# Attention with a gated convolution: the first query chunk of the first batch shares its weights with the last two chunks; tile 24 of v and small loads of v are fetched in another way

## The chip, the cores and the metric

The kernel runs on one core of one Trainium2 chip. The metric is the device time of one execution in microseconds (us), the median of several runs; lower is better. The engines are named as the profile names them: PE is TensorE with PEld for its weight loads, DVE is VectorE, ACT is ScalarE, POOL is GpSimd, and SP is SyncE, which here only issues DMA transfers (rows "SPq"). Every engine works through its own instructions strictly in order.

## The reference

Eight batches of 3200 rows. Per batch the scores of z with itself are scaled, cut off at zero and squared; this symmetric 3200 x 3200 matrix multiplies v, the result is multiplied by u, and the product x passes through a gate (a causal convolution of five taps and a sigmoid) and two 256 x 256 matrices:

```
scores = (1 / S) * z @ z.T            # z: 8 x 3200 x 64
attn   = maximum(scores, 0) ** 2      # symmetric
x      = u * (attn @ v)               # u, v: 8 x 3200 x 256
gate   = sigmoid(causal_conv5(x, conv_w))
out    = (gate * (x @ w_val)) @ w_out
```

## The kernel before

**Precision.** Every factor of a product is split into a high part, rounded to the format that PE takes, and a low part, the difference. A product is three matmuls (low x high, high x low, high x high). The names ending in `h`/`l` or `hi`/`lo`, and `v_hl` and `zhl`, which hold both, are these parts.

**Tiling.** The 3200 rows are 25 tiles of 128. Queries are handled in six chunks of four tiles (512 queries, `c` = 0 to 5), and the 25th tile (`ONE`) runs beside chunk 5. Keys are taken in pairs of tiles, `i` = 0 to 12; pair 12 is the single tile 24. Pairs 2c and 2c+1 lie in chunk c. One **step** is one (batch, chunk, pair).

**A step.** PE makes the scores of a step three steps ahead (`scores`, six matmuls into a bank `s`). `weights_of` turns them into weights: ACT cuts off and scales (L640, out of `s` into a buffer `a`, of which there are two), squares (L641) and rounds to `ah` (L643); DVE subtracts to get `al` (L649). Three steps later PE multiplies `ah` and `al` with v into the two banks `acc` (`attend`, 24 matmuls). All PE matmuls of a step have line L428 or L733, the helpers.

**Turned blocks.** Because the matrix is symmetric, the block (keys of chunk g, queries of chunk c) is the transpose of a block needed later, when chunk g is the query chunk. Where `keeps(b, c, g)` says so, `turn` has DVE transpose `a` into a tile `turned` (L520; two buffers) behind `al`, `keep` writes it to DRAM as `mir` (L542, four DMAs of SP), and in chunk g `m_fetch` reads it back into a tile `m` (L551, L555; four buffers). Such a **fetched** step has no scores, no L640 and no L641; ACT casts `ah` straight from `m`. Fetches are issued six or seven steps ahead. In batches 1 to 7 every chunk keeps blocks for all later ones. In batch 0 chunk 0 keeps only the block for `ONE`, and chunk 1 those for chunks 2 and later.

**Order of the steps.** `MIRRORED_AT` and the mixes place fetched steps between computed ones. In batch 0 chunk 4 computes pairs 0, 1, 8, 10, 11, 12 and half of 9 and fetches 2 to 7; chunk 5 computes 12, 0, 10, 1 and half of 11 and fetches 2 to 9 and the three groups of `ONE` (`FIRST_MIX`; K is the single pair, O the own pairs, F fetched, C other computed, S a group of `ONE`). In batches 1 to 6 chunk 4 fetches 0 to 7 in one run of six and two more, and chunk 5 fetches 0 to 9 (`LAST_MIX`).

**Order of the rest.** Everything else is put at steps by hand: `at_step(s, fn, ...)`. For v: `v_load` reads it from DRAM (L356, four DMAs of 32 partitions each), `v_high` rounds it (L410, on DVE in batch 0 but for pair 1, on ACT later), `v_low` subtracts (L415, DVE). `V_LOAD` and `V_HIGH` hold the steps for batches 1 and up, counted from the start of chunk 5 of the batch before; tile 24 is read three steps in and rounded six steps in. In batch 0 `v_load_chunk` reads v of chunks 2 to 5 into the two `turned` buffers. z of the next batch is loaded by `Z_FROM`, counted from the start of that batch. `convert` and `convert_conv` turn the weights, given as 64-bit numbers, into 32-bit ones on DVE, in pieces spread over the first 25 steps, with temporaries in the `m` buffers.

**Between chunks.** When a chunk's last step is done, DVE multiplies both banks with u (`gated`, L763); the next chunk's matmuls into `acc` wait for that.

**The end.** The last chunk of the last batch is cut into a left and a right half of 256 columns, each for two halves h of the channels, behind `if s == END`; the code there is written out in the order in which each engine runs it.

Of the kernel before, what the change touches and what calls it, by code (L numbers as in the profile page):

```python
# [12 lines left out]
P = 128  # L13
# [4 lines left out]
def attn_glu_kernel(  # L18
# [260 lines left out]
    def keeps(b, c, g):  # L279

        return c < g and (b > 0 or c > 1 or (c == 1 and g >= 2) or g == ONE)
# [10 lines left out]
    FIRST_MIX = "KCOFFSCFFSFOSFFF"  # L292
# [3 lines left out]
    for b in range(B):  # L296
        for c in range(n_chunks):
# [5 lines left out]
            if c == n_chunks - 1:  # L303
                mix = FIRST_MIX if b == 0 else LAST_MIX[b == B - 1]
# [4 lines left out]
                    "C": [i for i in computed if i < own(c, 0)],  # L309
# [42 lines left out]
    def v_rows(dst, b, g, t, m):  # L352

        for a in range(P // BLK):
# [31 lines left out]
    def v_load_chunk(b, g):  # L386
        if g % 2 == 0:
            two[0] = sb.tile([P, 2, CW // P, D], F32, name="v_raws", tag="turned", bufs=2)
        v_load(b, range(firsts[g], firsts[g] + sizes[g]), two[0][:, g % 2])
# [22 lines left out]
    def v_low(b, i):  # L412
        for j, m, raw in v_parts(b, i):
            high, low = (vt[b, i][:, x, j : j + m] for x in range(2))
            nc.vector.tensor_tensor(low, raw, f32(high), op=ALU.subtract)  # L415
# [462 lines left out]
    def gate_part_low(b, c, e, cols, gv):  # L878
        gvh, gvl = (x[:, e, cols] for x in gvs[b, c])
        nc.vector.tensor_tensor(gvl, gv, f32(gvh), op=ALU.subtract)  # L880
# [427 lines left out]
    def fill_at(s, fn, *args):  # L1308
# [26 lines left out]
    Z_FROM = {b: (-53, -48, -41, -33, -22, -10, -15) if b > 1 else (-17, -40, -35, -31, -24, -9, -5) for b in range(1, B)}  # L1335
# [8 lines left out]
        (3, (24,), (1, 6)),  # L1344
# [3 lines left out]
        (16, (18, 19), None),  # L1348
    )
    V_HIGH = (7, 8, 9, 10, 11, 12, 13, 16, 17, 18, 14, 15, 6)  # L1350
# [120 lines left out]
    with tc.manual_schedule():  # L1471
# [13 lines left out]
        for s in range(min(todo), END + 1):  # L1485
# [86 lines left out]
            if s == END:  # L1572
# [7 lines left out]
                for cols in (left_, right):  # L1580
                    for h in range(DH):
# [6 lines left out]
                        else:  # L1588
                            nc.vector.tensor_tensor(sums[h], apart[h][:, : CW // 2], sums[h], op=ALU.add)
                            gated(b, c, h, cols, sums[h])  # L1590
                        x_high(b, c, one[h], cols)
# [7 lines left out]
                        conv(b, c, h, 0, nc.scalar.mul if (cols is left_) == (h == 1) else nc.vector.tensor_scalar_mul, cols)  # L1599
# [10 lines left out]
                for h in range(DH):  # L1610
                    value_part(b, c, h, left_, value_l)
                value_part(b, c, 0, right, value_r)
# [3 lines left out]
                project_whole(b, c - 1, two_banks(False))  # L1616
# [6 lines left out]
                for e in range(DH):  # L1623
                    gate_part_low(b, c, e, left_, lefts[e])
# [13 lines left out]
                project_tiles(b, c, (2, 3), rights)  # L1638
                one_project_whole(g, s_bank_pair(1 - next_s[0]))
                tiles_out(b, c, (2, 3), rights, ("ut", "turned"), (nc.vector.tensor_copy, nc.scalar.copy), (nc.scalar, nc.scalar))  # L1640
                one_out(g)

# [32 lines left out]
```

## Time and profile before

| | us |
|---|---|
| median of three runs | 2258.09 |
| the three runs | 2257.62, 2263.52, 2258.09 |
| the profiled execution, its own time | 2262.12 |
| its span in the profile | 2260.3 |
| busy: DVE | 1852.5 |
| busy: ACT | 1707.4 |
| busy: POOL | 76.6 |

The granted clock of PE is 1.00 in all but the last stretch of the trace. A row of the timeline gives the start, the duration, the engine, the line in the kernel, the operation with its tiles, and in brackets how long the engine stood idle before it and what ended that. Durations of neighbouring rows of one engine overlap a little, so distances from start to start say what an instruction costs its engine.

### The profile page before, as it was taken

The page shows a single profiled execution, that of the slowest core. Times are in us where ns is not written, and L with a number is a line of the kernel's source. Part 1 is how long each engine was busy: PE and PEld are TensorE (multiplying, and loading weights), DVE is VectorE, ACT ScalarE, POOL GpSimd, SP SyncE. Part 2 cuts the span into 40 slices and gives each one's busy share as a digit, 9 for nine tenths or more (in the row PEclk, how much of TensorE's full clock was granted, in tenths as well). Part 3 has the DMA queues.
Part 4 walks back from the last instruction along what each step waited for, and adds up shares of the span by engine and source line. Part 5 has one row for each costly group of instructions (what it writes and reads, how often), then busy time and mean ns, then how long its engine had stood idle before and what let it go on. Part 6 is the DMA issues. An engine that isn't in the chain of part 4 may idle for free.

```text
span 2260.3 us, 50037 instructions
## 1 busy us (share of the span) xinstructions
PE 2247.4 (99%) x20311; PEld 1911.3 (85%) x20311; DVE 1852.5 (82%) x2296; ACT 1707.4 (76%) x2145; POOL 76.6 (3%) x119
## 2 busy tenths in 40 slices
PE   9999999999999999999999999999999999999998
PEld 7888888889888988888988888888898888888888
DVE  8877788887889778887888968888788887888776
ACT  8987688766887668876688766987669776697764
POOL 0000000000000000000000000000000000000000
PEclk9999999999999999999999999999999999999999
DMA  5557857887677876788667776777858778677663
GB/s 123 117 135 159 205 136 164 184 197 205 150 163 181 189 200 150 169 185 193 182 164 168 189 185 177 166 177 183 206 144 184 173 181 206 148 184 172 170 179 98
DMA packets 700600, 386.61 MB, mean 171 GB/s; under 512 B 411856, under 2 KB 635088, under 8 KB 700368
## 3 DMA queue, kind: packets, MB, share of 16 engines
q1 hardware_dynamic: 699024, 383.01, 71.4%
q8 instruction: 159, 2.61, 0.5%
q14 instruction: 73, 0.60, 0.1%
q10 hardware_dynamic: 1344, 0.39, 0.1%
HBM read 211.82 MB, written 171.44 MB: 170 GB/s over the span
## 4 chain that ended last, share of the span: by engine, by line
PE 92%; SPq 2%; DVE 2%; DMA 2%; ACT 1%; issue 1%; ACTq 0%; DVEq 0%
PE acc L428 67%; PE s L428 12%; PE misc L428 11%; DMA m<-mir 1%; SPq L356 1%; DVE al L649 1%; PE acc L733 1%; SPq L161 1%; SPq L1044 0%; DVE gate L811 0%; DMA z_raw<-in_z_dram 0%; DMA v_raws<-in_v_dram 0%; ACT ah L643 0%; SPq L555 0%; DVE x L763 0%
## 5 line engine op out<-in xcount | busy, mean ns | idle before, releaser
L428 PE MATMUL acc<-ah,v_hl 64*128 64x512 f32 x9472 | 1606.9, 388 | 1.2 <-DVE x L763 0.6
L428 PEld LDWEIGHTS acc<-ah,v_hl 64*128 64x128 f32 x9472 | 942.9, 184 | 165.0 <-issue 1.5
L428 PE MATMUL acc<-al,v_hl 64*128 64x512 f32 x4736 | 965.0, 387 | 2.1 <-DVE al L649 2.0
L428 PEld LDWEIGHTS acc<-al,v_hl 64*128 64x128 f32 x4736 | 480.9, 184 | 83.6 <-DVE al L649 4.8
L649 DVE TENSOR_TENSOR al<-a,ah 128x1024 fp32r<-128x1024 f32 (+1 forms) x346 | 398.3, 1151 | 184.5 <-ACT ah L643 182.7
L640 ACT ACTIVATE a<-s 128x1024 f32<-128x1024 f32 (+1 forms) x346 | 333.0, 963 | 137.5 <-PE s L428 122.8
L643 ACT CAST ah<-m 128x1024 fp32r<-128x1024 f32 x254 | 264.9, 1047 | 154.4 <-PE acc L428 83.0
L641 ACT ACTIVATE a<-a 128x1024 f32<-128x1024 f32 (+1 forms) x346 | 347.7, 1005 | 11.0
L649 DVE TENSOR_TENSOR al<-m,ah 128x1024 fp32r<-128x1024 f32 x254 | 307.8, 1212 | 53.7 <-ACT ah L643 53.6
L643 ACT CAST ah<-a 128x1024 fp32r<-128x1024 f32 (+1 forms) x323 | 319.9, 990 | 10.2
L520 DVE STREAM_TRANSPOSE turned<-a 128x1024 f32<-128x1024 f32 (+1 forms) x278 | 318.5, 1146 | 0.1
L811 DVE SCALAR_TENSOR_TENSOR gate<-x,cw,gate 128x512 f32<-128x512 f32 (+1 forms) x392 | 284.7, 726 | 4.9 <-ACT gate L809 1.1
L428 PE MATMUL s<-zq,zhl 64*128 64x512 f32 (+1 forms) x1596 | 222.5, 378 | 1.6 <-DVE gv L1065 1.6
L428 PEld LDWEIGHTS s<-zq,zhl 64*128 64x128 f32 x1596 | 153.0, 184 | 30.0 <-DVE gv L1065 2.0
L763 DVE TENSOR_TENSOR x<-acc,ut 128x512 f32<-128x512 f32 (+1 forms) x96 | 61.4, 681 | 83.4 <-PE acc L428 70.5
L815 ACT ACTIVATE gate<-gate 128x512 f32<-128x512 f32 (+1 forms) x98 | 60.9, 622 | 71.1 <-DVE gate L811 70.8
L913 ACT CAST gvh<-gv 128x512 fp32r<-128x512 f32 x94 | 58.2, 620 | 38.0 <-DVE gv L909 37.9
L428 PE MATMUL misc<-xh,w_val_hi 64*128 64x512 f32 x376 | 77.2, 386 | 0.0
L428 PE MATMUL misc<-xh,w_val_lo 64*128 64x512 f32 x376 | 77.2, 386 | 0.0
L428 PE MATMUL misc<-xl,w_val_hi 64*128 64x512 f32 x376 | 77.2, 386 | 0.0
L428 PE MATMUL s<-v_hl,ah 64*128 64x512 f32 x400 | 76.3, 394 | 0.0
L909 DVE TENSOR_TENSOR gv<-misc,gate 128x512 f32<-128x512 f32 x94 | 64.5, 686 | 12.7 <-PE misc L428 8.3
(197 smaller groups left out, 2021.7 us busy)
## 6 DMA issues: line engine op xcount, KB each, us to landing
mir<-turned SPq DMA_DIRECT2D x460, 256.0 KB, 4.1
m<-mir SPq DMA_DIRECT2D x230, 512.0 KB, 4.9
u_raw<-in_u_dram SPq DMA_DIRECT2D x384, 64.0 KB, 3.5
mir<-turned SPq DMA_DIRECT2D x376, 64.0 KB, 2.5
m<-mir SPq DMA_DIRECT2D x94, 256.0 KB, 4.6
out_dram<-ob SPq DMA_DIRECT2D x152, 128.0 KB, 3.6
v_raws<-in_v_dram SPq DMA_DIRECT2D x100, 128.0 KB, 3.7
z_raw<-in_z_dram SPq DMA_DIRECT2D x182, 64.0 KB, 3.2
```

Of the source, the lines that this page charges most:

```text
L161: queues[i % len(queues)].dma_start(dst[i * BLK : (i + 1) * BLK], src[:, d0 : d0 + BLK].rearrange("(j c) r -> c j r", c=BLK),)
L428: ins = nc.tensor.matmul(out_, st[r], mv[r], start=first, stop=last)
L520: nc.vector.transpose(into[:, t : t + m], a[:, j * w : (j + m) * w].rearrange("p (t m x) -> p t m x", t=m, x=BLK))
L640: nc.scalar.activation(a[:, : n * w].rearrange("p (j x) -> p j x", j=2), s[:, :, :each], AF.Relu, scale=scale)
L641: nc.scalar.activation(a, a, AF.Square)
L643: nc.scalar.copy(hi, a)
L649: nc.vector.tensor_tensor(lo, a, f32(hi), op=ALU.subtract)
L763: nc.vector.tensor_tensor(x[:, h, HALO + cols.start : HALO + cols.stop], accs[b, c][h][:, cols] if with_ is None else with_, ut[b, c][:, h ...
L811: nc.vector.scalar_tensor_tensor(g, tap, cw[:, h, k : k + 1], g, op0=ALU.mult, op1=ALU.add)
L815: nc.scalar.activation(g, g, AF.Sigmoid)
L909: nc.vector.tensor_tensor(gv[:, :w], pvs[b, c][e][:, :w], gates[b, c][:, e, :w], op=ALU.mult)
L913: nc.scalar.copy(gvs[b, c][0][:, e, :w], gv_[b, c, e][:, :w])
```

## The change

- `keeps`: in batch 0 chunk 0 now also keeps its blocks for chunks 4 and 5. In chunk 0 pairs 8 to 11 are transposed (four more L520) and two blocks are written; chunks 4 and 5 fetch pairs 0 and 1. Both chunks then have the order of steps of batches 1 to 6, and `FIRST_MIX` goes.
- `v_load_chunk`: v of chunks 2 to 5 of batch 0 goes into `m` buffers, one per chunk.
- `v_rows`: a load of fewer than four tiles is one DMA per tile over 128 partitions, no longer four of 32 partitions.
- `v_low`: pairs 9 to 12 of batch 0 on POOL.
- Tile 24 of v in batches 1 to 7: read together with tiles 18 and 19 (step 16), rounded at step 19.
- `Z_FROM` of batch 1: z of chunk 0 two steps later, z of tile 24 fifteen steps earlier.
- The end: in two of the four parts the first tap runs on ACT ahead of the cast of x; `project_whole` moves ahead of the right half's value matmuls; two subtractions go to POOL; tile 2 and tile 3 are projected and stored apart, and tile 3 is copied by DVE.

```diff
-        return c < g and (b > 0 or c > 1 or (c == 1 and g >= 2) or g == ONE)
+        return c < g and (b > 0 or c > 1 or (c == 1 and g >= 2) or g >= 4)
...
-    FIRST_MIX = "KCOFFSCFFSFOSFFF"
...
-                mix = FIRST_MIX if b == 0 else LAST_MIX[b == B - 1]
+                mix = LAST_MIX[b == B - 1]
...
     def v_rows(dst, b, g, t, m):
 
+        if m < P // BLK:
+            for x in range(m):
+                k = firsts[g] * P
+                rows_ = v[b, k : k + sizes[g] * P, :].rearrange("(a t r) d -> t a r d", t=sizes[g], r=BLK)[t + x]
+                nc.sync.dma_start(dst[:, x], rows_)
+            return
...
     def v_load_chunk(b, g):
-        if g % 2 == 0:
-            two[0] = sb.tile([P, 2, CW // P, D], F32, name="v_raws", tag="turned", bufs=2)
-        v_load(b, range(firsts[g], firsts[g] + sizes[g]), two[0][:, g % 2])
+        v_load(b, range(firsts[g], firsts[g] + sizes[g]), sb.tile([P, CW // P, D], F32, name="v_raws", tag="m", bufs=4))
...
-            nc.vector.tensor_tensor(low, raw, f32(high), op=ALU.subtract)
+            (nc.gpsimd if b == 0 and i > 8 else nc.vector).tensor_tensor(low, raw, f32(high), op=ALU.subtract)
...
-    def gate_part_low(b, c, e, cols, gv):
+    def gate_part_low(b, c, e, cols, gv, engine=nc.vector):
         gvh, gvl = (x[:, e, cols] for x in gvs[b, c])
-        nc.vector.tensor_tensor(gvl, gv, f32(gvh), op=ALU.subtract)
+        engine.tensor_tensor(gvl, gv, f32(gvh), op=ALU.subtract)
...
-    Z_FROM = {b: (-53, -48, -41, -33, -22, -10, -15) if b > 1 else (-17, -40, -35, -31, -24, -9, -5) for b in range(1, B)}
+    Z_FROM = {b: (-53, -48, -41, -33, -22, -10, -15) if b > 1 else (-15, -40, -35, -31, -24, -9, -20) for b in range(1, B)}
...
-        (3, (24,), (1, 6)),
...
-        (16, (18, 19), None),
+        (16, (18, 19, 24), None),
     )
-    V_HIGH = (7, 8, 9, 10, 11, 12, 13, 16, 17, 18, 14, 15, 6)
+    V_HIGH = (7, 8, 9, 10, 11, 12, 13, 16, 17, 18, 14, 15, 19)
...
+                        on_scalar = (cols is left_) == (h == 1)
+                        if on_scalar:
+                            conv(b, c, h, 0, nc.scalar.mul, cols)
                         x_high(b, c, one[h], cols)
...
-                        conv(b, c, h, 0, nc.scalar.mul if (cols is left_) == (h == 1) else nc.vector.tensor_scalar_mul, cols)
+                        if not on_scalar:
+                            conv(b, c, h, 0, nc.vector.tensor_scalar_mul, cols)
...
+                project_whole(b, c - 1, two_banks(False))
                 value_part(b, c, 0, right, value_r)
...
-                project_whole(b, c - 1, two_banks(False))
                 lefts = [gate_part(b, c, e, left_, value_l, "a") for e in range(DH)]
...
-                    gate_part_low(b, c, e, left_, lefts[e])
+                    gate_part_low(b, c, e, left_, lefts[e], nc.gpsimd)
...
-                project_tiles(b, c, (2, 3), rights)
+                project_tiles(b, c, (2,), rights[:1])
+                tiles_out(b, c, (2,), rights[:1], ("ut",), (nc.vector.tensor_copy,), (nc.sync,))
                 one_project_whole(g, s_bank_pair(1 - next_s[0]))
-                tiles_out(b, c, (2, 3), rights, ("ut", "turned"), (nc.vector.tensor_copy, nc.scalar.copy), (nc.scalar, nc.scalar))
+                project_tiles(b, c, (3,), rights[1:])
                 one_out(g)
+                tiles_out(b, c, (3,), rights[1:], ("turned",), (nc.vector.tensor_copy,), (nc.scalar,))
```

The change adds seven lines above most of these places, so line numbers of the changed kernel are two higher in the middle of the program and more near its end.

Three places in the engines' orders follow. The first is DVE in batch 0, chunk 0, from the subtraction of pair 8 (`al`) on; `v_hl_513` and `v_hl_506` are v of pair 8, `v_hl_566` and `v_hl_562` that of pair 9, `cv_` names are those of the conversion. Before:

```order
L649 TENSOR_TENSOR al<-a,ah 128x1024
L215 STREAM_TRANSPOSE zz<-z_raw 128x128
L415 TENSOR_TENSOR v_hl_513<-v_raws,v_hl_513 128x512
L410 CAST v_hl_566<-v_raws 128x512
L106 TENSOR_SCALAR cv_rest<-cv_words_363 128x10
L108 SCALAR_TENSOR_TENSOR cv_rest<-cv_words_363,cv_rest 128x10
L649 TENSOR_TENSOR al<-a,ah 128x1024
L231 TENSOR_TENSOR zhl_611<-zz,zhl_611 128x128
L415 TENSOR_TENSOR v_hl_566<-v_raws,v_hl_566 128x512
L410 CAST v_hl_615<-v_raws 128x512
```

The same stretch of DVE now:

```order
L651 TENSOR_TENSOR al<-a,ah 128x1024
L522 STREAM_TRANSPOSE turned<-a 128x2x16x32
L215 STREAM_TRANSPOSE zz<-z_raw 128x128
L417 TENSOR_TENSOR v_hl_506<-v_raws,v_hl_506 128x512
L412 CAST v_hl_562<-v_raws 128x512
L106 TENSOR_SCALAR cv_rest<-cv_words_356 128x10
L108 SCALAR_TENSOR_TENSOR cv_rest<-cv_words_356,cv_rest 128x10
L651 TENSOR_TENSOR al<-a,ah 128x1024
L522 STREAM_TRANSPOSE turned<-a 128x2x16x32
L231 TENSOR_TENSOR zhl_608<-zz,zhl_608 128x128
L412 CAST v_hl_612<-v_raws 128x512
```

A transpose stands behind each `al`, and the subtraction of pair 9's v has gone to POOL. `cv_rest` now takes the `m` buffer in which v of pairs 8 and 9 was, so its first instruction waits for POOL's subtraction of pair 9, which itself waits for the cast just ahead of it.

The second place is ACT in chunk 4 of batch 0, from the first tap of the gate of chunk 3 on; `a` out of `s` and `a` out of `a` are the cut-off and the square of a computed step. Before:

```order
L809 ACTIVATE gate<-x,cw 128x512
L1020 COPY parked<-misc_2740 128x512
L643 CAST ah<-m 128x4x2x128
L809 ACTIVATE gate<-x,cw 128x512
L1020 COPY parked<-misc_2741 128x512
L640 ACTIVATE a<-s_2868 128x1024
L641 ACTIVATE a<-a 128x1024
L643 CAST ah<-a 128x1024
L226 CAST zhl_2917<-zz 128x512
L643 CAST ah<-m 128x4x2x128
L640 ACTIVATE a<-s_2935 128x1024
L641 ACTIVATE a<-a 128x1024
```

And now:

```order
L811 ACTIVATE gate<-x,cw 128x512
L645 CAST ah<-m 128x4x2x128
L811 ACTIVATE gate<-x,cw 128x512
L1022 COPY parked<-misc_2759 128x512
L1022 COPY parked<-misc_2760 128x512
L645 CAST ah<-m 128x4x2x128
L226 CAST zhl_2924<-zz 128x512
L645 CAST ah<-m 128x4x2x128 x2
L817 ACTIVATE gate<-gate 128x512
L645 CAST ah<-m 128x4x2x128 x2
```

Six fetched steps follow each other where fetched and computed ones took turns.

The third place is SP in chunk 5 of batch 0, from the first load of v for batch 1 on; `m` rows are fetches, and `mir_6` those of the groups of tile 24. Before:

```order
L356 DMA v_raws<-in_v_dram 32x4x256 x4
L555 DMA m<-mir_6_1994 128x4x128
L555 DMA m<-mir_6_2614 128x4x128
L356 DMA v_raws<-in_v_dram 32x256 x4
L555 DMA m<-mir_5_2510 128x4x256
L356 DMA v_raws<-in_v_dram 32x4x256 x4
L551 DMA m<-mir_5_3425 128x512
L555 DMA m<-mir_6_3140 128x4x128
L555 DMA m<-mir_6_3317 128x4x128
L356 DMA v_raws<-in_v_dram 32x4x256 x4
```

And now:

```order
L360 DMA v_raws<-in_v_dram 32x4x256 x4
L557 DMA m<-mir_6_2001 128x4x128
L557 DMA m<-mir_6_2621 128x4x128
L557 DMA m<-mir_5_2517 128x4x256
L360 DMA v_raws<-in_v_dram 32x4x256 x4
L553 DMA m<-mir_5_3408 128x512
L557 DMA m<-mir_6_3166 128x4x128
L557 DMA m<-mir_6_3292 128x4x128
L360 DMA v_raws<-in_v_dram 32x4x256 x4
```

The four small loads of tile 24 have left this place; they stand as one DMA behind tiles 18 and 19 at the start of batch 1.

More of the change, by code (lines that the diff above doesn't have):

```diff
@@ L308, in attn_glu_kernel @@
                     "F": fetched,
-                    "C": [i for i in computed if i < own(c, 0)],
                     "S": list(range(NT // GROUP)),
```

## The prediction

> **What bounds the kernel now.** I read the busy times first, then the stretches, then the ends of the chunks.
>
> ```profile
> span 2260.3 us, 50037 instructions
> ...
> PE 2247.4 (99%) x20311; PEld 1911.3 (85%) x20311; DVE 1852.5 (82%) x2296; ACT 1707.4 (76%) x2145; POOL 76.6 (3%) x119
> ```
>
> PE works 2247.4 of 2260.3 us. So two things shorten this program: fewer matmuls, or less of the 12.9 us in which PE stands still. An engine beside PE counts only where PE waits for it. The table of stretches, taken over the seam between two batches (columns: stretch, its length, busy PE, PEld, DVE, ACT, POOL, granted clock, DMA share, GB/s), shows where PE stands still:
>
> ```profile
> 240.00:292.00 52.00, 49.12 (x446) 43.41 (x444) 39.72 (x52) 30.78 (x41) 1.28 (x2) 1.00 0.78 193
> 520.00:572.00 52.00, 52.00 (x492) 50.89 (x490) 43.17 (x59) 34.30 (x46) 1.28 (x2) 1.00 0.75 194
> ```
>
> The first row is the seam from batch 0 to batch 1, the second that from batch 1 to batch 2. PE idles 2.88 us in the one and nothing in the other. The ends of the chunks show it with all side effects: `x`, DVE's product behind a chunk's last matmul (L763, timeline of DVE).
>
> ```profile
> 194.66 1.29 DVE L763 TENSOR_TENSOR x<-acc,ut 128x512 f32<-128x512 f32 x2 [1.20 <-PE acc L428]
> ...
> 239.29 1.29 DVE L763 TENSOR_TENSOR x<-acc,ut 128x512 f32<-128x512 f32 x2 [4.32 <-PE acc L428]
> ...
> 295.44 1.29 DVE L763 TENSOR_TENSOR x<-acc,ut 128x512 f32<-128x512 f32 x2 [0.53 <-PE acc L428]
> ...
> 477.63 1.29 DVE L763 TENSOR_TENSOR x<-acc,ut 128x512 f32<-128x512 f32 x2 [3.08 <-PE acc L428]
> ...
> 519.99 1.29 DVE L763 TENSOR_TENSOR x<-acc,ut 128x512 f32<-128x512 f32 x2 [3.28 <-PE acc L428]
> ...
> 571.10 1.29 DVE L763 TENSOR_TENSOR x<-acc,ut 128x512 f32<-128x512 f32 x2 [1.16 <-PE acc L428]
> ...
> 1632.58 1.29 DVE L763 TENSOR_TENSOR x<-acc,ut 128x512 f32<-128x512 f32 x2 [3.28 <-PE acc L428]
> ...
> 1685.07 1.29 DVE L763 TENSOR_TENSOR x<-acc,ut 128x512 f32<-128x512 f32 x2 [1.23 <-PE acc L428]
> ...
> 2150.14 1.29 DVE L763 TENSOR_TENSOR x<-acc,ut 128x512 f32<-128x512 f32 x2 [2.16 <-PE acc L428]
> ...
> 2192.50 1.29 DVE L763 TENSOR_TENSOR x<-acc,ut 128x512 f32<-128x512 f32 x2 [3.28 <-PE acc L428]
> ```
>
> Each row marks the end of a chunk. Chunk 4 takes 239.29 - 194.66 = 44.63 us in batch 0, and 42.36 in batch 1 (519.99 - 477.63) as in batch 7 (2192.50 - 2150.14), the first and the last of seven. Chunk 5 takes 56.15 in batch 0 (295.44 - 239.29), 51.11 in batch 1 (571.10 - 519.99), and 52.49 in batch 5, the longest of the later ones (1685.07 - 1632.58).
>
> **Chunks 4 and 5 of batch 0.** The change gives both the order of steps of batch 1. Two computed steps in each become fetched, so four groups of six score matmuls go. What one group costs stands in PE's timeline:
>
> ```profile
> 250.60 0.92 PE L428 MATMUL s<-zhl,zhl 64*128 64x512 f32 x6
> 251.30 0.45 PE L428 MATMUL acc<-ah,v_hl 64*128 64x512 f32 x2
> ```
>
> From start to start 0.70 us; four make 2.80. Scores run three steps ahead, so three groups leave the interval of chunk 4 and one that of chunk 5. Three groups are 2.10, and the row distance of chunk 4 says 44.63 - 42.36 = 2.27; I take **-2.27** for chunk 4, between 2.1 and 2.3. In chunk 5 one group is 0.70 for certain. The rest of its excess is the stall, which PE's waits from 230 to 300 us name:
>
> ```profile
> PE s L428 <- DVE gv L1065: 1.6, 1, 1.6
> PE acc L428 <- DVE al L649: 0.8, 1, 0.8
> ```
>
> PE waits for DVE there, DVE for ACT's casts, and ACT stands in front of a load:
>
> ```profile
> 267.31 0.41 ACT L410 CAST v_hl<-v_raws 128x256 fp32r<-128x256 f32 x1 [7.08 <-DMA v_raws<-in_v_dram]
> ```
>
> That is tile 24 of batch 1, rounded three steps after SP was told to read it. ACT loses 7.08 us, and the casts of the fetched steps queue behind it. The change takes this cast out of the stretch and four DMA issues out of SP's queue; it puts in four `m` fetches over both chunks and, at the start of chunk 5, the four z loads that stood two steps earlier. ACT loses two pairs of L640 and L641 in each chunk, which it need not do at all. What is late next is a fetch, as in batch 1, where PE shows no idle. I expect 51.5 us for chunk 5, near 51.11 and a little above it for the z load that batch 1 has not: **-4.65**, with ends -0.70 (only the scores go) and -5.04.
>
> **Later seams.** The cast of tile 24 moves in every batch. In batches 1 to 6 PE hardly idles at that place, so it can win little: batch 5's chunk 5 is 1.38 over batch 1's, and I credit half, **-0.7** (0 to -1.4). At its new place, three steps into the next batch, ACT spends the 0.41 us of the row above, which a computed step's slack covers; without that cover it would cost 0.4 in each of seven batches.
>
> **Chunk 0 of batch 0, which pays for it.** PE has no idle there, so the question is what DVE can carry before PE waits for it at the end of the chunk. DVE's slack in the stretch is the idle time ahead of these rows:
>
> ```profile
> 39.02 1.23 DVE L649 TENSOR_TENSOR al<-a,ah 128x1024 fp32r<-128x1024 f32 x1 [0.45 <-ACT ah L643]
> ...
> 40.37 0.68 DVE L415 TENSOR_TENSOR v_hl<-v_raws,v_hl 128x512 fp32r<-128x512 f32 x1
> ...
> 42.33 1.22 DVE L649 TENSOR_TENSOR al<-a,ah 128x1024 fp32r<-128x1024 f32 x1 [0.85 <-ACT ah L643]
> ...
> 45.43 1.23 DVE L649 TENSOR_TENSOR al<-a,ah 128x1024 fp32r<-128x1024 f32 x1 [0.94 <-ACT ah L643]
> ...
> 51.95 1.22 DVE L649 TENSOR_TENSOR al<-a,ah 128x1024 fp32r<-128x1024 f32 x1 [0.76 <-ACT ah L643]
> ...
> 55.64 1.29 DVE L763 TENSOR_TENSOR x<-acc,ut 128x512 f32<-128x512 f32 x2 [0.33 <-PE acc L428]
> ...
> 68.12 1.24 DVE L520 STREAM_TRANSPOSE turned<-a 128x1024 f32<-128x1024 f32 x1
> ```
>
> The sum of the five is 0.45 + 0.85 + 0.94 + 0.76 + 0.33 = 3.33 us. The change adds four transposes of 1.24 (the last row), 4.96, and takes away three subtractions of v of 0.68 (the row at 40.37) and one of half that width, 2.38. It also adds a wait: `cv_rest` now waits for POOL's subtraction of pair 9, and behind it on DVE stand the next `al`, and behind that PE. What POOL needs for such an operation, and what it does to DVE, stands in two rows of the seam to batch 2:
>
> ```profile
> 603.56 1.29 POOL L1084 TENSOR_TENSOR one_sum<-one_sum,one_f 128x512 f32<-128x512 f32 x1 [29.99 <-DMA one_f<-in_u_dram]
> 603.59 2.35 DVE L649 TENSOR_TENSOR al<-a,ah 128x1024 fp32r<-128x1024 f32 x1
> ```
>
> POOL takes 1.29 us over 128x512. The `al` that starts 0.03 us after it takes 2.35 instead of 1.23: it stood 1.12 us. So far DVE is later by 4.96 - 2.38 + 1.29 = 3.87. Three more POOL subtractions follow, each released by the cast of v in front of an `al`; whether `al` stands depends on who starts first. Behind the cast of pair 10 there is one small operation ahead of `al`, so POOL can be first there; behind that of pair 11 `al` follows at once and starts first. I count one such stand, 1.12. DVE is then 4.99 late, 3.33 of it covered: `x` of chunk 0, and PE with it, is late by **+1.7**. The ends are 0.5 (no `al` stands: 3.87 - 3.33) and 3.9 (three do), and 0 if ACT's waits, too, were only PE's pace. [...]
>
> The v loads move into `m` buffers, and one of them, that of chunk 5, now waits until DVE has subtracted pair 7's v:
>
> ```profile
> 34.05 0.69 DVE L415 TENSOR_TENSOR v_hl<-v_raws,v_hl 128x512 fp32r<-128x512 f32 x1
> ...
> 40.97 0.42 DVE L410 CAST v_hl<-v_raws 128x512 fp32r<-128x512 f32 x1
> ```
>
> The first row is that subtraction, the second the first cast that reads the load.
>
> ```profile
> v_raws<-in_v_dram SPq DMA_DIRECT2D x100, 128.0 KB, 3.7
> ```
>
> Released at 34.74, four issues and 3.7 us of landing bring it near 40.4, ahead of 40.97, and the cast itself moves later by the first transposes. Behind it on SP stand u, tile 24 and the first kept block, all read later. I count nothing; each us of lateness beyond would come on top of the 1.7. The two blocks written and read again are 2 MB each way beside a DMA share of 0.78 at most: nothing. The loads of v in fewer DMAs leave SP earlier, but at the start PE's first product waits for DVE's rounding of the weights, not for v: nothing.
>
> ```profile
> 10.75 0.73 PE L428 MATMUL acc<-ah,v_hl 64*128 64x512 f32 x4 [0.53 <-DVE ah L579]
> ```
>
> **The end.** Here DVE is the chain. Two parts begin with this:
>
> ```profile
> 2239.66 0.41 ACT L794 CAST xh<-x 128x256 fp32r<-128x256 f32 x1 [0.76 <-DVE x L763]
> 2239.97 0.51 ACT L809 ACTIVATE gate<-x,cw 128x256 f32<-128x256 f32 x1
> ```
>
> On DVE, in the same stretch:
>
> ```profile
> 2235.06 0.42 DVE L763 TENSOR_TENSOR x<-acc,ut 128x256 f32<-128x256 f32 x1 [1.02 <-PE acc L728]
> ...
> 2235.99 2.46 DVE L811 SCALAR_TENSOR_TENSOR gate<-x,cw,gate 128x256 f32<-128x256 f32 x4
> ...
> 2240.51 2.05 DVE L811 SCALAR_TENSOR_TENSOR gate<-x,cw,gate 128x256 f32<-128x256 f32 x4 [0.55 <-ACT gate L809]
> ...
> 2251.16 0.75 DVE L880 TENSOR_TENSOR gvl<-gv,gvh 128x256 fp32r<-128x256 f32 x2
> ```
>
> With the first tap ahead of the cast, DVE starts its four taps 2239.97 - 2239.66 = 0.31 us sooner, twice: 0.62. Two subtractions (0.75) leave DVE for POOL, but POOL beside DVE's taps can cost: one set of four taps took 2.46, another 2.05, 0.41 more. 0.62 + 0.75 - 0.41 = **-1.0** (0 to -2.0: the copies and the projection of tile 3 in another order may add as much again). SP's last issue closes the chain:
>
> ```profile
> 2256.69 0.66 SPq L1267 DMA_DIRECT2D out_dram<-one_f  x1
> ```
>
> **The sum.** -2.27 - 4.65 - 0.7 + 1.7 - 1.0 = -6.9 us. The profiled execution took 2262.12 (1.8 around its span), which would become 2255.2. It lies 4.0 above the median of the runs shown, so of the median, 2258.09, I forecast 2251.2, which is -0.31%.
>
> **The rivals.**
> - *Every POOL subtraction blocks DVE* (chunk 0). Three stands instead of one, +2.2: 2253.4. For it: the 2.35 row. Against it: `al` is issued at once behind one of the casts.
> - *Chunk 5 keeps its stall* and loses only the 0.70, because z of batch 1 and the fetches crowd SP's queue where tile 24 left it; the change then does not do there what it is made of. 3.95 is missing: 2255.2. Against it: batch 1's seam with the same order and no idle PE.
> - *The long run of fetched steps starves PE* in chunks 4 and 5, and the kernel is slower. The chain of waits has the price of one late fetch:
>
> ```profile
> 282.23 4.29 DMA m<-mir
> ```
>
>   It landed 4.29 us after its issue and ended in PE's wait of 1.6 us. If each of the 16 fetched pairs of both chunks cost that, 25.6 us come on top: 2276.8. The turning point is 6.9 / 16 = 0.43 us for each. Against it stand seven chunks 4 of 42.36 us with this very run.
>
> **How the numbers follow.** My forecast has 0.66, with 2247.5 to 2253.5 as its own range; the rivals have 0.14, 0.13 and 0.07. A measurement of this kernel tells about 0.3% from no change, that is 6.8 us, or 2251.3: the forecast lies on that edge. Of its 0.66 I give 0.42 to faster and 0.24 to within; of the first rival 0.03 and 0.11; of the second 0.01 and 0.12; of the third 0.05 to slower and 0.02 to within. Faster 0.46, within 0.49, slower 0.05. The range from 2246.5 to 2257.5 takes in both small rivals and the open ends of the terms, and leaves out the third.
>
> **What would show it.** In the changed profile the distances of `x` rows should be 42.4 us for chunk 4 and about 51.5 for chunk 5 of batch 0, and PE's idle time from 240 to 292 us below 1 us. `x` of chunk 0 should stand near 57.3 instead of 55.64; at 56.2 no `al` stood, at 59.5 three did. From `x` at 2235.06 to the end of the span it was 25.2 us and should be about 24.2. The forecast is wrong if chunk 5 stays above 54 us, if a DVE cast in chunk 0 waits for v from DRAM, or if PE waits for casts of `m` in chunk 4.

## The result, and the profile after

The changed kernel takes 2277.82 us (median of six runs, 2276.20 to 2282.03) against 2258.52 of the kernel before beside it: the ratio is 1.0085, 95% interval 1.0072 to 1.0098. It became slower where the forecast had -0.3%.

The page of after, its span and busy times:

```profile
span 2276.1 us, 49896 instructions
...
PE 2250.2 (99%) x20287; PEld 1908.4 (84%) x20287; DVE 1856.8 (82%) x2294; ACT 1698.5 (75%) x2137; POOL 83.6 (4%) x125
```

PE has 24 matmuls fewer and a span 15.8 us longer, and not 19.3, because the profiled execution of before was 4.0 us above its median. The ends of the chunks say where that lies (DVE's timeline of after; the end of chunk 3, 4 and 5 of batch 0 behind that of chunk 0, then both ends of batch 6's chunk 5):

```profile
61.02 1.28 DVE L765 TENSOR_TENSOR x<-acc,ut 128x512 f32<-128x512 f32 x2
...
199.98 1.29 DVE L765 TENSOR_TENSOR x<-acc,ut 128x512 f32<-128x512 f32 x2 [0.55 <-PE acc L430]
...
242.40 1.29 DVE L765 TENSOR_TENSOR x<-acc,ut 128x512 f32<-128x512 f32 x2 [2.60 <-PE acc L430]
...
301.86 1.29 DVE L765 TENSOR_TENSOR x<-acc,ut 128x512 f32<-128x512 f32 x2 [0.51 <-PE acc L430]
...
1924.51 1.29 DVE L765 TENSOR_TENSOR x<-acc,ut 128x512 f32<-128x512 f32 x2 [3.28 <-PE acc L430]
...
1980.76 1.29 DVE L765 TENSOR_TENSOR x<-acc,ut 128x512 f32<-128x512 f32 x2 [1.25 <-PE acc L430]
```

The distances, against the forecast:

| part | before | after | difference | forecast |
|---|---|---|---|---|
| chunk 0 of batch 0, to its `x` | 55.64 | 61.02 | +5.38 | +1.7 |
| chunk 4 of batch 0 | 44.63 | 42.42 | -2.21 | -2.27 |
| chunk 5 of batch 0 | 56.15 | 59.46 | +3.31 | -4.65 |
| chunks 5 of batches 1 to 6 together | 309.30 | 318.37 | +9.07 | -0.7 |
| from the last `x` to the end of the span | 25.24 | 25.46 | +0.22 | -1.0 |

These five make 15.8, so every other chunk is as long as before. Of the six later chunks 5, those of batches 2, 3, 5 and 6 are 1.4 to 4.9 us longer, the other two within 0.9. Chunk 4 came out to 0.06 us; all else is off, and the three large differences lie where v is loaded. The start of the program shows it first. In the table of stretches of after (columns: stretch, its length, busy PE, PEld, DVE, ACT, POOL, granted clock, DMA share, GB/s) PE all but stops, and then the clock falls:

```profile
9.00:10.50 1.50, 0.01 (x1) 0.04 (x1) 0.94 (x2) 0.28 (x1) 0.00 (x0) 1.00 0.29 89
10.50:12.00 1.50, 0.62 (x4) 0.38 (x4) 1.50 (x4) 0.09 (x1) 0.00 (x0) 0.91 0.47 116
12.00:13.50 1.50, 1.23 (x6) 0.96 (x8) 1.43 (x4) 1.47 (x3) 0.00 (x0) 0.50 0.47 119
13.50:15.00 1.50, 1.50 (x10) 1.11 (x10) 1.50 (x4) 1.47 (x4) 0.00 (x0) 0.50 0.47 120
```

The timelines of DVE and PE name what they waited for; the first row is that cast in the kernel before, the others are of after:

```profile
6.65 0.43 DVE L410 CAST v_hl<-v_raw 128x512 fp32r<-128x512 f32 x1
...
9.53 0.43 DVE L412 CAST v_hl<-v_raw 128x512 fp32r<-128x512 f32 x1 [2.75 <-DMA v_raw<-in_v_dram]
...
10.49 0.63 PE L202 MATMUL misc<-ident,z_rows 128*128 128x128 f32 x4 [1.81 <-DMA z_rows<-in_z_dram]
12.27 1.22 PE L430 MATMUL acc<-ah,v_hl 64*128 64x512 f32 x4 [1.15 <-DVE ah L581]
```

The cast of the first v stood at 6.65 us in the kernel before and waited for nothing. SP had begun to issue that load at 3.05 us before and at 3.07 after. PE's 1.81 us are for a load of z that was issued behind the first two loads of v. At the seams the same lateness falls on the fetches that share SP's queue. The waits of after, then of before (engine, line and tile, what it waited for: us in total, times, longest):

```profile
ACT ah L645 <- DMA m<-mir: 120.5, 54, 6.7
```

```profile
ACT ah L643 <- DMA m<-mir: 53.8, 41, 4.4
```

In after ACT waits more than twice as long for fetched blocks, for a fetch that is as large and as frequent as before in batches 1 to 6.

### The profile page after: what moved, and what is told of

It reads as the page before. It is cut to its first block, busy times and chain, and to the rows that moved or that the text cites. A ratio compares the mean times of both kernels' runs of the same rounds, so it can differ in the third digit from the quotient of the medians.

```text
span 2276.1 us, 49896 instructions
## 1 busy us (share of the span) xinstructions
PE 2250.2 (99%) x20287; PEld 1908.4 (84%) x20287; DVE 1856.8 (82%) x2294; ACT 1698.5 (75%) x2137; POOL 83.6 (4%) x125
## 4 chain that ended last, share of the span: by engine, by line
PE 87%; DMA 6%; DVE 3%; SPq 2%; ACT 1%; issue 1%; DVEq 0%; POOL 0%; POOLq 0%; ACTq 0%
PE acc L430 64%; PE s L430 11%; PE misc L430 11%; DMA m<-mir 3%; DMA v_raws<-in_v_dram 1%; DVE al L651 1%; DMA v_raw<-in_v_dram 1%; SPq L161 1%; ACT ah L645 1%; DVE gate L813 1%; PE acc L735 1%; SPq L360 0%; DMA z_raw<-in_z_dram 0%; DVE x L765 0%; DMA out_dram<-ob 0%
## 5 line engine op out<-in xcount | busy, mean ns | idle before, releaser
L651 DVE TENSOR_TENSOR al<-a,ah 128x1024 fp32r<-128x1024 f32 x342 | 394.0, 1152 | 188.6 <-ACT ah L645 187.2
L645 ACT CAST ah<-m 128x1024 fp32r<-128x1024 f32 x258 | 269.3, 1047 | 218.3 <-DMA m<-mir 120.5
L642 ACT ACTIVATE a<-s 128x1024 f32<-128x1024 f32 x342 | 328.9, 962 | 131.7 <-PE s L430 115.5
L651 DVE TENSOR_TENSOR al<-m,ah 128x1024 fp32r<-128x1024 f32 x258 | 312.7, 1212 | 59.9 <-ACT ah L645 59.8
L643 ACT ACTIVATE a<-a 128x1024 f32<-128x1024 f32 x342 | 343.5, 1004 | 10.9
L522 DVE STREAM_TRANSPOSE turned<-a 128x1024 f32<-128x1024 f32 (+1 forms) x282 | 323.1, 1146 | 0.0
```

Of the source, the lines that this page charges most:

```text
L522: nc.vector.transpose(into[:, t : t + m], a[:, j * w : (j + m) * w].rearrange("p (t m x) -> p t m x", t=m, x=BLK))
L642: nc.scalar.activation(a[:, : n * w].rearrange("p (j x) -> p j x", j=2), s[:, :, :each], AF.Relu, scale=scale)
L643: nc.scalar.activation(a, a, AF.Square)
L645: nc.scalar.copy(hi, a)
L651: nc.vector.tensor_tensor(lo, a, f32(hi), op=ALU.subtract)
```

## The experiments

Theory V: the new small loads of v land late and hold up what is queued behind them. Rivals: W, the moved load of tile 24 collides at the seams; X, batch 0's long run of fetched steps starves PE. Four runs tell them apart, each undoing or doing one part.

**e1_old_rows.** The kernel after, without this piece of `v_rows`:

```diff
-        if m < P // BLK:
-            for x in range(m):
-                ...
-                nc.sync.dma_start(dst[:, x], rows_)
-            return
```

> The kernel after, with one part undone: every load of fewer than four tiles of v again goes out as four DMAs of 32 partitions, not as one DMA of 128 partitions per tile. Theory V (the new form lands late and holds up what is queued behind it): chunk 0 of batch 0 returns from 61.0 to about 57.5 us (the 1.7 us of the transposes stay), the last chunks of batches 1 to 6 lose the 9.1 us that they gained, the last chunk of batch 0 falls from 59.5 us; in all about 2263 us. Theory W (the moved load of tile 24 collides at the seams): only chunk 0 gets better, about 2274 us. Theory X (the long fetched run of batch 0 starves TensorE): only chunk 0 gets better too, about 2274 us.

2263.66 us, 1.0013 of before (1.0004 to 1.0023): 14.2 us below after. Chunk 0 3.4 us shorter (57.65), chunk 5 of batch 0 3.2 (56.23), those of batches 1 to 6 together 7.4 (311.01). ACT's wait for fetched blocks falls from 120.5 to 89.0 us. V holds; W and X would have left 2274.

**e2_new_rows_alone.** The same piece, added to the kernel before.

> The kernel before, with one part of the change alone: loads of fewer than four tiles of v as one DMA of 128 partitions per tile. Theory V: slower by 3.5 us in chunk 0 and by some 9 us in the last chunks of batches 1 to 6, about 2271 us, and more waits of ScalarE for fetched blocks (m<-mir) than the 53.8 us of before. Theory W: chunk 0 alone, about 2262 us. Theory X: the same, about 2262 us.

2283.19 us, 1.0104 (1.0087 to 1.0121), and ACT waits 102.4 us for `m<-mir`. Chunk 0 is 3.0 us longer than before (58.68), as I had it to 0.5; chunks 5 of batches 1 to 6 are 15.2 longer (324.47) where I had 9. V again, and dearer than I said.

**e3_old_tile24 and e4_new_tile24_alone.** In the kernel after the load of tile 24 goes back, in the kernel before it is moved:

```diff
-        (16, (18, 19, 24), None),
+        (3, (24,), (1, 6)),
+        (16, (18, 19), None),
```

> The kernel after, with one part undone: v's 25th tile of the next batch is loaded at step 3 and cast at step 6 again, not at steps 16 and 19. Theory W: the last chunks of batches 1 to 6 lose the 9.1 us they gained, about 2268 us. Theory V: no change within 3 us, about 2278 us. Theory X: no change, about 2278 us.

> The kernel before, with one part of the change alone: v's 25th tile of the next batch is loaded at step 16 and cast at step 19. Theory W: slower by some 9 us in the last chunks of batches 1 to 6, about 2267 us. Theory V: no change within 3 us, about 2258 us. Theory X: no change, about 2258 us.

2282.40 and 2262.90 us (1.0102, 1.0084 to 1.0120; 1.0013, 1.0004 to 1.0023). W falls as the main cause. Moving tile 24 has a small price by itself, 3 us; beside the slow loads it rather saves (4.6 us between the medians, though the intervals overlap; I had said within 3).

Why do they land late? The loads have the same bytes in rows of 1 KB, and fewer DMAs. In the kernel after, a source is four groups of 32 rows that lie apart (the `a` and `r` of the rearranged v), its target 128 partitions; the old form was 32 partitions at a time, each group by itself. Only the groups of tile 24 adjoin: in batch 0 of after its one DMA, issued at 38.24 us, moves most of its 128 rows from 40.5 to 41.0 us (230 GB/s, a DMA share of 0.68). Two runs change the shape of the source.

**e5_contiguous_source.**

```diff
-                rows_ = v[b, k : k + sizes[g] * P, :].rearrange("(a t r) d -> t a r d", t=sizes[g], r=BLK)[t + x]
-                nc.sync.dma_start(dst[:, x], rows_)
+                nc.sync.dma_start(dst[:, x], v[b, k + (t + x) * P : k + (t + x + 1) * P, :])
```

> The kernel after, with the small loads of v still one DMA of 128 partitions per tile, but read from 128 rows that follow one another in DRAM, not from four groups of 32 rows: the number of DMAs, partitions, bytes and row lengths are the same, and batches get other rows of v, so the output differs. Theory K (the split of the source into four groups lets the DMA run on few of the 16 DMA engines): as fast as with the old loads, about 2264 us, chunk 0 near 57.7 us. Theory N (a DMA of 128 partitions per tile is slow as such, or fewer DMAs hold up the queue): stays at about 2278 us, chunk 0 near 61 us.

2257.78 us, 0.9986 (0.9976 to 0.9995), chunk 0 57.00, and chunk 5 of batch 0 51.70, what the forecast had. This kernel reads other rows of v than the reference wants, so only its time is of use. It says that neither 128 partitions nor a DMA per tile is slow, and that without the grouped sources all of the 19.3 us come back (2277.82 - 2257.78 = 20.0).

**e6_two_halves.**

```diff
-                nc.sync.dma_start(dst[:, x], rows_)
+                for y in range(2):
+                    nc.sync.dma_start(dst[y * P // 2 : (y + 1) * P // 2, x], rows_[2 * y : 2 * y + 2])
```

> The kernel after, with each small load of v cut into two DMAs of 64 partitions, the source of each two groups of 32 rows; the same data. Theory K (the number of groups in the source sets how many DMA engines work): both halves run on two engines each, half as many as before, so the extra time of the small loads doubles or more: 2290 to 2310 us, chunk 0 beyond 64 us. Theory N (128 partitions in one DMA are slow): 64 partitions are nearer to the old 32, so faster than after, 2264 to 2275 us.

2359.90 us, 1.0447 (1.0418 to 1.0476): theory K in direction, and dearer than its number. Stretches near the start in which almost nothing but the 1 KB rows of small loads of v is moved show the mean busy share of the 16 DMA engines and what they move (share and GB/s at the end of the row; a packet counts whole in the stretch in which it starts, so a share can pass 1). The rows are of after, of e6_two_halves, of e5_contiguous_source and of before:

```profile
10.00:11.00 1.00, 0.51 (x4) 0.42 (x4) 1.00 (x2) 0.00 (x0) 0.00 (x0) 1.00 0.27 91
```

```profile
13.00:15.00 2.00, 0.90 (x6) 0.67 (x6) 1.97 (x4) 0.84 (x2) 0.00 (x0) 0.68 0.14 46
```

```profile
8.00:8.50 0.50, 0.50 (x8) 0.40 (x6) 0.10 (x1) 0.42 (x2) 0.00 (x0) 1.00 1.03 356
```

```profile
9.00:10.00 1.00, 1.00 (x10) 0.60 (x6) 1.00 (x2) 0.97 (x2) 0.00 (x0) 1.00 0.45 139
```

From four groups the share is 0.27 at 91 GB/s, from two 0.14 at 46, from 128 rows in a row 1.03 at 356. In e6_two_halves a tile is two DMAs, and still the share is 0.14. The old form reaches 0.45 and 139 GB/s there, near what SP issues: eight loads of 64 KB in 3.90 us are 134 GB/s (SP's timeline of before, from 6.39 us).

At 91 GB/s two tiles, 256 KB, take 2.9 us; at 356 they take 0.7 (an estimate from these two rates). Sixteen times 0.27 and 0.14 is 4.3 and 2.2, near the four and the two groups; that so many engines work is an estimate from the shares. Why a source in groups has this effect, the runs do not show.

**e7_old_rows_old_tile24 and e8_old_rows_old_z.** Two small suspects on top of e1_old_rows: tile 24 as before; `Z_FROM` of batch 1 as before.

> The kernel after with the old small loads of v, and also with v's 25th tile loaded at step 3 and cast at step 6 again. If the move of that tile costs what it cost alone (about 3 us: 1.5 in the last chunk of batch 0, 1.3 in that of batch 5), about 2260.5 us with the last chunk of batch 0 near 54.7 us. If the move is what made that chunk shorter after all and the 56.2 us come from elsewhere, 2264 us or more.

> The kernel after with the old small loads of v, and with batch 1's two moved loads of z put back (first chunk's 17 steps ahead of the batch, not 15; the last one's 5 steps ahead, not 20). Theory Z (the four z loads that stand ahead of the first two m fetches in the last chunk of batch 0, 2.73 us of SP's queue, start its lateness): that chunk falls from 56.2 to about 53.4 us, total about 2261 us. Theory F (fetches land late because the whole chunk is fetched, whatever stands in SP's queue there): 56 us and 2264 us or more.

2260.34 us (0.9997, 0.9988 to 1.0007) and 2261.53 (1.0002, 0.9992 to 1.0013). Against e1_old_rows that is 3 us for the move of tile 24, as before, and 2 for that of z; both intervals still overlap with that of e1_old_rows. Chunk 5 of batch 0 takes 55.50 and 55.08 us, not the 54.7 and 53.4 that I had expected.

**e9_whole_chunks and e10_before_whole_chunks.** The right data without a grouped source: at the seams whole chunks of four tiles are loaded.

```diff
-        if m < P // BLK:
+        if sizes[g] == 1:
...
-        (-6, (14, 15, 16, 17), None),
+        (-6, (16, 17, 18, 19), None),
...
-        (8, (12, 13), (1, 4)),
-        (16, (18, 19, 24), None),
+        (8, (12, 13, 14, 15), (1, 4)),
+        (16, (24,), None),
```

> The kernel after with the same number of loads of v, all of them with a source that does not fall into four groups: at the seams whole chunks of four tiles are loaded (16 to 19 at step -6 and 12 to 15 at step 8, in four DMAs of 32 partitions each, in place of 14 to 17, 12 to 13 and 18 to 19), tile 24 stays one DMA, batch 0's pairs are four DMAs again. Theory K (few DMA engines made the small loads late, and the smaller count of DMAs is what the last chunk of batch 0 needs): as with the contiguous source, chunk 0 57 to 57.7 us, last chunk of batch 0 51.5 to 52.5 us, 2257 to 2259 us, below the kernel before. Theory D (the contiguous rows themselves, not the engines, made that run fast): last chunk of batch 0 near 56 us, 2263 us.

> The kernel before with only the loads of v of the run e9_whole_chunks (and tile 24 at step 16). If fewer DMAs at the seam alone took the stall out of the last chunk of batch 0: that chunk below 54 us and about 2256 us, with the kept blocks worth only the 2.2 us of chunk 4. If the computed steps of that chunk need the kept blocks to get faster: 56 us and 2259 to 2262 us.

2286.09 and 2293.03 us (1.0118, 1.0103 to 1.0133; 1.0142, 1.0125 to 1.0159): missed. Chunk 0 (56.66) and chunk 5 of batch 0 (53.18) of e9_whole_chunks are nearer to theory K than to D, but the first chunk of every later batch is 1.0 to 4.4 us longer. The waits of e9_whole_chunks say why:

```profile
DVE turned L522 <- DMA mir<-turned: 36.3, 9, 5.9
```

Tiles 14 and 15 lie in a `turned` buffer until their cast at step 16, and the transposes of the next batch lack it. In e10_before_whole_chunks chunk 5 of batch 0 takes 57.07: in this one profile fewer loads alone did not shorten it.

**e11_conv_rest_apart and e12_lows_on_vector** ask what chunk 0 costs: `cv_rest` gets its own buffer; then pairs 9 to 12 go back to DVE.

> The run e9_whole_chunks with one thing more: the small tile cv_rest gets a buffer of its own, so that VectorE no longer waits 1.4 us for GpSimd to free an m buffer in chunk 0 of batch 0. If that wait is on the path, as the forecast's sum for chunk 0 had it, x of chunk 0 comes 1.3 us earlier, 55.7 to 56.4 us. If VectorE has slack there: no change, 57 us.

> The run e11_conv_rest_apart with the subtractions for v's later pairs in batch 0 back on VectorE, none on GpSimd. The forecast's sum for chunk 0: four subtractions more on VectorE cost 2.5 us, against one al that no longer takes 2.31 us in place of 1.22 and two shorter operations beside it: x of chunk 0 1 to 1.5 us later than in e11_conv_rest_apart. If the operations that GpSimd blocks are dearer than the work it takes over: earlier than there.

2308.62 and 2304.96 us (1.0213 and 1.0199, each within 0.0016): something else. Chunks 1 to 4 of every batch grew by 0.3 to 0.9 us. The groups of instructions from 60 to 240 us (count, busy us, mean ns, idle before), of e9_whole_chunks and of e11_conv_rest_apart:

```profile
L430 PE MATMUL acc<-ah,v_hl 64*128 64x512 f32 x772 | 128.8, 389 | 0.0
```

```profile
L430 PE MATMUL acc<-ah,v_hl 64*128 64x512 f32 x768 | 128.6, 391 | 0.0
```

The same matmul takes 2 ns more once a tile of 40 bytes a partition stands among the others.

**f13_early_casts** casts tiles 12 to 15 at steps 12 and 13; **f14_rest_padded** adds `cv_rest` in 256 bytes of its own; **f15_padded_lows_vector** puts all subtractions on DVE; **f16_all_mended** also puts z back.

```diff
-    V_HIGH = (7, 8, 9, 10, 11, 12, 13, 16, 17, 18, 14, 15, 19)
+    V_HIGH = (7, 8, 9, 10, 11, 12, 12, 13, 17, 18, 14, 15, 19)
```

> The run e9_whole_chunks with the casts of tiles 12 to 15 at steps 12 and 13, not 13 and 16, so that the buffer of turned blocks in which they land is free again as early as in the kernel after. If the held buffer is what made the first chunk of every batch 1 to 4 us longer there: the 23.6 us it had over the contiguous source up to the last batch go, 2257 to 2260 us, last chunk of batch 0 near 52 us. If whole-chunk loads are late for another reason: 2275 us or more.

> The run f13_early_casts with cv_rest in a buffer of its own of 256 bytes a partition. Theory A (the 40-byte tile put the others at addresses at which TensorE reads slower): chunks 1 to 4 return to 46.57 and 42.42 us. Rival (any further tile does it): 46.9 and 42.9. Chunk 0: if VectorE's wait for GpSimd is on the path, x 1.3 us earlier than in f13_early_casts; if not, within 0.4.

> The run f14_rest_padded with all subtractions of v's pairs on VectorE in batch 0. By the forecast's sum x of chunk 0 1 to 1.5 us later than in f14_rest_padded. If the operations that GpSimd blocks are dearer than the work it takes over, as the blurred runs hint: 0.5 to 1 us earlier, total 2255 to 2258 us.

> The run f15_padded_lows_vector with batch 1's two moved loads of z put back to 17 and 5 steps ahead. If they cost as beside the old loads of v (last chunk of batch 0 1.1 us, of batch 1 1.1 us): 2 us less than f15_padded_lows_vector, 2253 to 2256 us. If fewer loads of v in SP's queue leave room for them: no change.

2263.51, 2265.53, 2263.63 and 2259.38 us (1.0015, 1.0023, 1.0015, 0.9997, each within 0.001). The held buffer was the cause of the first chunks: they are back at 47.9 us. With 256 bytes chunks 1 to 4 take 46.54 to 42.42 us again. But f13_early_casts, f15_padded_lows_vector and f16_all_mended lie 3.4 to 5.6 us above the ranges that I had given, and f14_rest_padded shows one way in which such time goes. PE's timeline, and its stretches:

```profile
288.08 1.65 PE L430 MATMUL s<-zq,zhl 64*128 64x512 f32 x6 [2.83 <-DVE gv L1067]
```

```profile
286.00:290.00 4.00, 1.92 (x10) 1.55 (x12) 3.77 (x6) 3.38 (x6) 0.00 (x0) 0.66 0.00 0
290.00:294.00 4.00, 4.00 (x22) 3.16 (x20) 3.96 (x7) 2.35 (x3) 0.00 (x0) 0.50 0.07 14
```

One wait of 2.83 us, and the granted clock is 0.66 in the stretch in which it ends and 0.50 in the next 4 us. Its eleven runs fall into two at 2258 to 2260 and nine at 2265 to 2269 us; the profiled one is of the nine, and that the clock parts the two groups is not shown. Nor does a long wait always bring this. In e2_new_rows_alone the same step waits 3.26 us (PE's timeline), and the clock behind it stays at 1.00:

```profile
295.19 0.96 PE L434 MATMUL s<-zq,zhl 64*128 64x512 f32 x6 [3.26 <-DVE gv L1071]
```

```profile
296.00:300.00 4.00, 4.00 (x38) 3.32 (x36) 3.96 (x8) 3.19 (x5) 0.00 (x0) 1.00 0.01 4
```

In f13_early_casts, on the other hand, the clock is 0.50 from 60 to 62 us behind a wait of 1.82 us, and chunk 1 takes 48.15 us where the other runs have 46.5 to 46.9. In f16_all_mended PE has no idle in chunk 5 of batch 0 (stretch from 238 to 290 us):

```profile
238.00:290.00 52.00, 52.00 (x488) 49.50 (x486) 43.61 (x58) 34.30 (x45) 2.18 (x2) 1.00 0.80 193
```

It takes 51.41 us there, but 313.4 in batches 1 to 6, against 309.3 before.

**f17_first_seam and f18_first_seam_old_loads** keep batch 0 as in f16_all_mended and leave the later seams as before; the second has no whole chunks at the first seam either. In both v of chunks 2 to 5 of batch 0 still goes into `m` buffers.

> The run f16_all_mended with the whole-chunk loads of v (and the late tile 24) at the first seam alone; the seams of batches 2 to 7 load v as the kernel before does, with tile 24 as one DMA. If the whole-chunk loads cost the 4 us by which the last chunks of batches 1 to 6 were longer in f16_all_mended than before, and the gain in batch 0 is real: 2253 to 2256 us, last chunk of batch 0 51 to 54 us, those of batches 1 to 6 at 308 to 310 us together. If the short last chunk of f16_all_mended was luck of one execution: 2257 to 2260 us.

> The run f17_first_seam with all loads of v as before, tile 24 at step 3: the kernel after with its kept blocks and its last steps, cv_rest apart, and nothing else of the change in batch 0. If fewer DMAs at the first seam are what shortens the last chunk of batch 0: that chunk 54.5 to 56 us, 2257 to 2259 us, 2 to 4 us above f17_first_seam. If they are not: the same as f17_first_seam within a microsecond.

2259.56 and 2258.03 us (0.9995, 0.9986 to 1.0004; 0.9988, 0.9979 to 0.9997). Chunk 5 of batch 0 takes 53.40 and 56.19 us in their profiles, yet the medians go the other way, within their intervals, and the profiled executions are unlike ones: 2257.50 us, below its kernel's median, and 2261.76, the longest of its kernel's. Whether fewer DMAs at the first seam help isn't settled. These two undo what hurts and keep the blocks: they beat the kernel after by 0.8 to 0.9%, and the kernel before by 0.12% at most. The interval of f18_first_seam_old_loads just leaves out 1, that of f17_first_seam doesn't.

## Why the prediction was wrong, by its own steps

- **The step that failed** is "The loads of v in fewer DMAs leave SP earlier ...: nothing". I counted DMAs and not the shape of their source. Of the 19.3 us lost (2277.82 - 2258.52) the old loads give back 14.2 (e1_old_rows) and contiguous sources all (e5_contiguous_source); that run and e6_two_halves show that the four groups are the cause. The rest of the change gave no -6.9 either: against the kernel before beside them these two runs stand at +3.9 and -3.2 us. I also argued with the wrong cover: "PE's first product waits for DVE's rounding of the weights, not for v" held only as long as v was early, and "if a DVE cast in chunk 0 waits for v from DRAM" was the sign that came.
- **Chunk 4, -2.27**: right, -2.21, and 42.42 in nearly every run that keeps the blocks.
- **Chunk 5 of batch 0, -4.65**: only possible, not steady. Without grouped sources and with kept blocks thirteen single profiles give 51.4 to 58.1 us, 54.8 in the mean: -1.4 against the one profile of before, -2.2 against the mean of the three with the blocks not kept (56.15, 57.68 and 57.07). Where PE hardly stands still the forecast's 51.5 is met (51.70 with 0.11 us of idle, 51.41 with none); in the other eleven PE stands 1.6 to 3.7 us, the second rival, a seam that keeps some of its stall. What decides it from run to run stays open, beyond the clock step that f14_rest_padded shows.
- **Later seams, -0.7**: wrong sign. Tile 24 at its new place costs about 3 us (e4_new_tile24_alone; e1_old_rows against e7_old_rows_old_tile24), mostly in chunks 5 of single batches.
- **Chunk 0, +1.7**: right in sum. DVE's added work begins behind the `al` of pair 8 (before, then after):

```profile
35.93 1.23 DVE L649 TENSOR_TENSOR al<-a,ah 128x1024 fp32r<-128x1024 f32 x1 [0.69 <-ACT ah L643]
```

```profile
39.46 1.22 DVE L651 TENSOR_TENSOR al<-a,ah 128x1024 fp32r<-128x1024 f32 x1 [0.70 <-ACT ah L645]
```

  From there to `x` it is 19.71 us before and 21.56 after: +1.85. The other 3.53 of the 5.38 us stand ahead of that `al` and come from the late start. The parts were less right. DVE's wait for POOL, counted 1.29 us, is worth 0.4: without it the stretch takes 21.18 us in f14_rest_padded, because there the next small operation stands beside POOL in its place, 1.29 us where it took 0.17. One long `al` stood, as counted, but beside the subtraction of pair 11 and not of pair 10: at pair 11 POOL started at 50.29 us and `al` at 50.35, and `al` took 2.31 us in place of 1.22; at pair 10 `al` started at 47.52 us and took 1.22, and POOL, from 47.61 us, took 2.29 in place of 1.29 (timelines of after). In f14_rest_padded a DVE instruction took longer beside two of POOL's four subtractions (timelines of POOL and of DVE):

```profile
39.66 1.30 POOL L417 TENSOR_TENSOR v_hl<-v_raws,v_hl 128x512 fp32r<-128x512 f32 x1 [37.65 <-DVE cv_rest L106]
...
46.54 1.30 POOL L417 TENSOR_TENSOR v_hl<-v_raws,v_hl 128x512 fp32r<-128x512 f32 x1 [0.39 <-DVE v_hl L412]
```

```profile
39.69 1.29 DVE L108 SCALAR_TENSOR_TENSOR cv_rest<-cv_words,cv_rest 128x10 f32<-128x10 uint32 x1
...
46.61 2.31 DVE L651 TENSOR_TENSOR al<-a,ah 128x1024 fp32r<-128x1024 f32 x1 [0.15 <-ACT ah L645]
```

  POOL's subtractions, which I credited with 2.38 us of relief, cost in the end: with all of them on DVE the stretch takes 20.4 us in the last four runs, 0.75 less than in f14_rest_padded.
- **The end, -1.0**: it was +0.2. DVE's taps did start sooner, their idle of 0.55 twice became 0.30 and 0.24. POOL's two subtractions stood beside DVE's work, and of that the last three taps took 1.84 us against 1.52 (timelines of POOL and DVE of after, then DVE of before):

```profile
2264.41 1.45 POOL L882 TENSOR_TENSOR gvl<-gv,gvh 128x256 fp32r<-128x256 f32 x2 [1.93 <-ACT gvh L877]
```

```profile
2265.34 1.84 DVE L813 SCALAR_TENSOR_TENSOR gate<-x,cw,gate 128x256 f32<-128x256 f32 x3
```

```profile
2249.73 1.52 DVE L811 SCALAR_TENSOR_TENSOR gate<-x,cw,gate 128x256 f32<-128x256 f32 x3
```

  DVE's last product for the store of `one_f` still came 0.58 us sooner behind the last chunk's first `x`: 20.60 us (2271.24 - 2250.64) against 21.18 (2256.24 - 2235.06). SP gave that away. It has three stores of `ob_tile` ahead of that store where it had two (timelines of SP, after and before), and comes to it 1.2 us after the product is ready, where before it came at once:

```profile
2270.80 1.96 SPq L898 DMA_DIRECT2D out_dram<-ob_tile  x3
2272.86 0.56 SPq L1269 DMA_DIRECT2D out_dram<-one_f  x1
```

```profile
2254.90 1.54 SPq L896 DMA_DIRECT2D out_dram<-ob_tile  x2
```
- **The third rival** gave 2276.8, near the time measured, by another mechanism: chunk 4, with its run of fetched steps, lost nothing, so the nearness is luck. Its sum also counts 16 fetched pairs where the two chunks have 8 and 10; with 18 it is 2280.0. The chance of "slower" was too small because a slow load was no case at all.

## What to carry to other kernels

Before a load is merged into fewer DMAs, look at how its source lies in DRAM: here DMAs of one tile to 128 partitions each ran at a DMA share of 0.27 and 91 GB/s from a source in four groups, and at 1.03 and 356 GB/s from 128 rows in a row. A change at a seam where PE has little idle has little to win there and, here, 9 us to lose; one wait of 2.83 us came with 6.8 us at a granted clock of 0.50, and one of 3.26 us with none. Work moved to an idle engine was no relief here: beside it `al` took 2.31 us in place of 1.22. Read such a chunk in several executions, since single ones of 51 to 58 us were all of nearly the same program.

## What the runs showed of the hardware

- The small loads: a DMA share of 0.27 from four groups of 32 rows (after) and of 1.03 from 128 rows in a row (e5_contiguous_source), where the source alone differs; 0.14 from halves with two groups each (e6_two_halves).
- With waits of 1.81 and 1.15 us in one place (after, 10.5 to 12.3 us) and of 2.83 us in another (f14_rest_padded), PE's granted clock was 0.50 for 3.4 and for 6.8 us, worked out from the rows of stretches there. Behind 2.27 us (after, 296.0 us) and 3.26 us (e2_new_rows_alone) it stayed at 1.00, so the length of the wait alone does not tell. In batch 6's chunk 5 of after, which takes 56.25 us, it was 0.63 from 1968 to 1972 us, behind waits of 0.97, 0.90 and 0.77 us (PE's timeline, 1962.18 to 1967.38 us).
- With a tile of 40 bytes a partition among the others the same matmuls took 391 ns in place of 389 (e11_conv_rest_apart, e9_whole_chunks), and chunks 1 to 4 of each batch 0.3 to 0.9 us more; with one of 256 bytes they took 389 (f14_rest_padded). That the addresses are the cause was not tried by itself.
